# One plain feature tile instead of two, and eighteen early products instead of ten, in a Strassen-Winograd GeGLU kernel

## The chip, the cores and the metric

The kernel runs on one core of one Trainium2 chip. The metric is the device time of a run in microseconds (us). Most kernels' runs here lie within some 0.4% of each other, and only a comparison against the kernel before, run on the same chip in the same rounds, is used for small differences.

PE is the matmul engine (TensorE), PEld its weight loads, DVE is VectorE, ACT is ScalarE, POOL is GpSimd, SP is SyncE, which here only issues DMAs. `ps...` names are banks of PSUM, the memory that the matmuls write; SBUF is the memory that holds their operands.

## The reference

```python
# x: 1024 tokens x 1024, w_gate, w_up: 1024 x 3584, w_down: 3584 x 1024, all bf16
def reference(x, w_gate, w_up, w_down):
    return (gelu_tanh(x @ w_gate) * (x @ w_up)) @ w_down
```

## The kernel before

The features come in 28 tiles of 128. For each tile the kernel needs gate and up for 1024 tokens: plainly, 2 matrices x 2 token blocks x 8 depth steps = 32 matmuls of 128x512. Nearly all tiles are done by the Strassen-Winograd scheme instead. Depth and tokens are each cut in two, so w_gate gives the quadrants a11, a12, w_up gives a21, a22, and x transposed gives b11, b12, b21, b22. Seven products of four matmuls replace eight: 28 matmuls a tile. Its price is sums: s1 to s4 of weights (on DVE for the first pair, on POOL for all later ones) and t1 to t4 of x (on DVE), in fp32r, a 4-byte type.

A first few tiles stay plain, because they need no sums and can run while x and weights still arrive. Besides them, the product a12 x b21 (called P2) needs no sums either. It is computed early ("ahead") for some tiles, copied to SBUF, and added back when the tile's turn comes. Before, two tiles are plain and ten have P2 ahead. The code is shortened, and comments are added.

```python
FC = 2                       # tiles of a pair ("chunk")
NAHEAD = 10                  # tiles whose P2 is kept ahead
...
for k, eng in enumerate((nc.sync, nc.scalar)):        # start of the loads
    load_ahead(0, k, k + 1, eng)
for which, eng in enumerate((nc.sync, nc.scalar)):
    load_w(eng, 0, which, KD, KD + KQ)
load_xT(0, KD + KQ, DT)      # transposing DMA of x
load_ahead(0, KQ, KD)
load_w0(nc.sync, KD + KQ, DT)
load_ahead(1, 0, KD)
load_xT(0, 0, KD)
load_w0(nc.sync, 0, KD)
load_xT(1, 0, KD)
load_xT(1, KD, DT)
...                          # then w_up, w_gate of the first pair, last a12 rows
for ci in range(1, NCH):     # the pairs
    ...
    for fl in range(FC): prod(psc[fl], s1[fl], t1, True)    # the first product with sums
    for fl in range(FC): prod(psa[fl], s2[fl], t2, False)
    for st in open_fts: last_product(st)                    # a22r x t4 of the pair before
    for fl, ft in enumerate(fts): prod(psc[fl], s4[fl], b22r, False)
    if fts[0] < FC + NAHEAD: h0 = first                     # P2 was kept ahead
    else: ...                                               # P2 now, in a B bank
    begun = [first_product(ft + FC) for ft in fts]          # a11 x b11 of the next pair
    for fl, ft in enumerate(fts): prod(psa[fl], s3[fl], t3, False)
```

## Time and profile before

| | before |
|---|---|
| time, median | 275.52 us of the first 3 runs; 275.12 of the 6 that the change was compared with |
| profiled execution | span 273.2 us (time 274.97) |
| PE busy | 268.9 us, 98% |
| first pair: w_up and w_gate landed (issue plus time to landing) | 23.4 and 24.1 us |
| first pair: first weight load of a11 x b11 | 25.1 us |

These lines are from the page of the kernel before: busy time by engine, busy tenths in 40 slices, and the chain that ended last, by engine.

```profile
PE 268.9 (98%) x1202; PEld 188.4 (69%) x1202; DVE 193.8 (71%) x194; ACT 112.1 (41%) x183; POOL 107.1 (39%) x55
...
PE   8999999999999999999999999999999999999994
...
DMA  7994321423505505050514280005992445696202
...
PE 98%; ACT 0%; issue 0%
```

PE has work in every slice, and the chain from the last instruction back to the first is PE almost alone. So only fewer matmuls can make it shorter, and a new wait of PE makes it longer. DMA is fully busy only in the start, up to some 20 us, and from 191 to 205 us.

The table by stretches of 10 us, of the kernel before; after the length come busy us and instructions of PE, PEld, DVE, ACT and POOL, then the granted clock, the DMA share and GB/s. The DMA share sums the packets' own times, so it can exceed 1.

```profile
0.00:10.00 10.00, 9.23 (x43) 4.45 (x44) 1.27 (x3) 3.05 (x5) 0.70 (x6) 1.00 0.93 221
10.00:20.00 10.00, 10.00 (x48) 4.56 (x47) 5.09 (x6) 4.67 (x7) 0.00 (x0) 1.00 0.99 232
20.00:30.00 10.00, 10.00 (x47) 4.89 (x46) 9.16 (x8) 3.81 (x6) 0.00 (x0) 1.00 0.63 177
```

In the start both PE and DMA are full.

The chain in order of time, kernel before (start us, length us, what; L257 are products of the scheme, L272 the P2 ahead):

```profile
25.50 1.73 PE psA L257 x8
27.23 1.73 PE psC L272 x8
28.96 1.92 PE psC L257 x8
30.88 1.83 PE psA L257 x8
...
269.75 0.58 ACT o_sb L571
```

Eight bf16 matmuls take 1.73 us, 0.216 each; in the fp32r products eight take 1.81, 0.226 each. The piece at 28.96 is s1 x t1 of the first pair, the first product that needs sums. It divides the start from the rest (the timeline has its start at 28.77).

### The profile page before, as it was taken

The page shows a single profiled execution, that of the slowest core. Times are in us where ns is not written, and L with a number is a line of the kernel's source. Part 1 is how long each engine was busy: PE and PEld are TensorE (multiplying, and loading weights), DVE is VectorE, ACT ScalarE, POOL GpSimd, SP SyncE. Part 2 cuts the span into 40 slices and gives each one's busy share as a digit, 9 for nine tenths or more (in the row PEclk, how much of TensorE's full clock was granted, in tenths as well). Part 3 has the DMA queues.
Part 4 walks back from the last instruction along what each step waited for, and adds up shares of the span by engine and source line. Part 5 has one row for each costly group of instructions (what it writes and reads, how often), then busy time and mean ns, then how long its engine had stood idle before and what let it go on. Part 6 is the DMA issues. An engine that isn't in the chain of part 4 may idle for free.

```text
span 273.2 us, 3351 instructions
## 1 busy us (share of the span) xinstructions
PE 268.9 (98%) x1202; PEld 188.4 (69%) x1202; DVE 193.8 (71%) x194; ACT 112.1 (41%) x183; POOL 107.1 (39%) x55
## 2 busy tenths in 40 slices
PE   8999999999999999999999999999999999999994
PEld 4444777877877677676868686754447888888883
DVE  0268997986655676766658556459999999999511
ACT  2262665454643646555463636430300023962001
POOL 1000099999796794949577575000000000000000
PEclk9999999999999999999999999999999999999999
DMA  7994321423505505050514280005992445696202
GB/s 189 239 258 133 105 71 44 118 62 94 156 14 140 146 8 157 0 154 3 153 36 119 57 291 1 0 2 163 353 292 79 132 137 187 217 284 196 78 0 78
DMA packets 53249, 33.77 MB, mean 124 GB/s; under 512 B 8688, under 2 KB 53232, under 8 KB 53232
## 3 DMA queue, kind: packets, MB, share of 16 engines
q1 hardware_dynamic: 50240, 31.07, 39.7%
q10 hardware_dynamic: 2992, 2.49, 2.8%
q8 instruction: 9, 0.15, 0.2%
q14 instruction: 8, 0.07, 0.1%
HBM read 29.62 MB, written 2.10 MB: 116 GB/s over the span
## 4 chain that ended last, share of the span: by engine, by line
PE 98%; ACT 0%; issue 0%
PE psA L257 34%; PE psA L431 18%; PE psC L257 17%; PE psC L431 7%; PE psB L431 7%; PE psB L257 5%; PE psB L239 3%; PE psA L239 3%; PE psC L272 2%; PE psA L272 1%; PE psA L224 1%; PE tp L232 0%; ACT o_sb L571 0%
## 5 line engine op out<-in xcount | busy, mean ns | idle before, releaser
L257 PE MATMUL psA<-t,s 128*128 128x512 f32 x208 | 54.2, 402 | 0.0
L249 ACT ACTIVATE h<-c 128x512 bf16<-128x512 f32 x52 | 31.7, 627 | 37.4 <-DVE c L335 37.4
L257 PEld LDWEIGHTS psA<-t,s 128*128 128x128 f32 x208 | 39.1, 188 | 9.3
L162 POOL TENSOR_TENSOR s<-wu 128x1024 fp32r<-128x1024 bf16 x12 | 26.1, 2179 | 25.0 <-PE psC L257 16.8
L335 DVE TENSOR_TENSOR c<-sn,psA 128x512 f32<-128x512 f32 x26 | 17.7, 682 | 16.5 <-PE psA L257 14.6
L257 PEld LDWEIGHTS <-wg 128*128 128x128 bf16 x168 | 15.4, 98 | 20.2 <-issue 3.4
L163 POOL TENSOR_TENSOR s<-s,wg 128x1024 fp32r<-128x1024 f32 x12 | 27.4, 2284 | 0.9
L165 POOL TENSOR_TENSOR s<-wg,wu 128x1024 fp32r<-128x1024 bf16 x12 | 27.1, 2255 | 0.0
L340 ACT COPY sn<-psA 128x512 f32<-128x512 f32 x42 | 23.7, 584 | 7.9 <-PE psA L257 7.8
L257 PE MATMUL psA<-t,a22r 128*128 128x512 f32 x104 | 25.9, 391 | 0.0
L257 PE MATMUL psC<-t,s 128*128 128x512 f32 x104 | 25.8, 390 | 0.0
L257 PE MATMUL psC<-b22r,s 128*128 128x512 f32 x104 | 25.7, 389 | 0.0
L340 ACT COPY sn<-psC 128x512 f32<-128x512 f32 x26 | 15.2, 588 | 24.5 <-PE psC L257 22.7
L257 PE MATMUL psA<-b,wg 128*128 128x512 bf16 x104 | 24.6, 380 | 0.0
L257 PEld LDWEIGHTS psC<-t,s 128*128 128x128 f32 x104 | 19.4, 188 | 4.4 <-ACT ahead L362 0.3
L257 PEld LDWEIGHTS psA<-t,a22r 128*128 128x128 f32 x104 | 19.5, 188 | 4.1
L257 PEld LDWEIGHTS psC<-b22r,s 128*128 128x128 f32 x104 | 19.5, 188 | 4.1
L335 DVE TENSOR_TENSOR c<-sn,psC 128x512 f32<-128x512 f32 x26 | 17.7, 687 | 6.2 <-PE psC L257 6.2
L354 DVE TENSOR_TENSOR hi<-h,psA 128x512 bf16<-128x512 bf16 x14 | 9.6, 687 | 13.2 <-PE psA L257 13.2
L164 POOL TENSOR_TENSOR s<-wg,s 128x1024 fp32r<-128x1024 bf16 x8 | 17.2, 2155 | 0.6
L410 DVE TENSOR_TENSOR lo<-c,h 128x512 bf16<-128x512 f32 x12 | 16.9, 1405 | 0.6
L410 DVE TENSOR_TENSOR hi<-c,h 128x512 bf16<-128x512 f32 x14 | 16.9, 1205 | 0.5
(95 smaller groups left out, 398.5 us busy)
## 6 DMA issues: line engine op xcount, KB each, us to landing
wu<-in_w_up_dram SPq DMA_DIRECT2D x13, 512.0 KB, 4.1
wdb<-in_w_down_dram SPq DMA_DIRECT2D x12, 512.0 KB, 4.7
wdb<-in_w_down_dram SPq DMA_DIRECT2D x12, 384.0 KB, 4.2
wg<-in_w_gate_dram SPq DMA_DIRECT2D x8, 512.0 KB, 5.2
v<-in_w_down_dram SPq DMA_DIRECT2D x4, 512.0 KB, 6.1
out_dram<-o_sb ACTq DMA_DIRECT2D x16, 128.0 KB, 1.7
wg<-in_w_gate_dram SPq DMA_DIRECT2D x6, 256.0 KB, 4.5
v<-in_w_down_dram SPq DMA_DIRECT2D x4, 384.0 KB, 7.4
```

The lines of the kernel that those rows point to most:

```text
L162: yield eng.tensor_tensor(s1, a21, a22, ADD)
L163: yield eng.tensor_tensor(s2, s1, a11, SUB)
L164: yield eng.tensor_tensor(s4, a12, s2, SUB)
L165: yield eng.tensor_tensor(s3, a11, a21, SUB)
L239: nc.tensor.matmul(ps, lhsT=w_tiles[0, which][:, dt, fl * P : (fl + 1) * P], rhs=x_rows(dt, nb), start=(dt == first), stop=(dt == last),)
L249: nc.scalar.activation(h, src, ACT.Gelu_apprx_tanh)
L257: nc.tensor.matmul(ps, lhsT=lhs[:, k, :], rhs=rhs[:, k, :], start=(start and k == 0), stop=(k == KD - 1), skip_group_check=True,)
L335: tt(t, s, ps, ADD)
L340: nc.scalar.copy(t, ps)
L354: tt(g_of(ft)[:, :NB], h0, psa, MUL)
L410: tt(g_of(ft)[:, NB:], added(sn5[fl], psa[fl]), h1[fl], MUL)
L431: nc.tensor.matmul(banks[m], lhsT=lhs(k)[:, m * P : (m + 1) * P], rhs=rhs(k), start=(start and k == 0), stop=(k == HF - 1), skip_group_che ...
```

## The change

One tile less is plain, so one tile more saves its four matmuls. What PE loses in the start is made up by keeping P2 of eight more tiles ahead, eighteen in all. The results lie in SBUF rows of g that are not written yet (those of the first four in its lower half, the others in its upper half, as before), and the a12 rows of the later ten lie in slots of later sums. The 28 tiles become one plain tile, thirteen pairs and one last tile alone. The diff, cut to its core:

```diff
-    NCH = FT // FC
-    NAHEAD = 10
+    chunks = [range(0, 1)] + [range(f0, min(f0 + FC, FT)) for f0 in range(1, FT, FC)]
+    NCH = len(chunks)
+    NAHEAD = 18
...
+        a12_ahead += [
+            spool.tile([P, KD, KB * P], bf16, name="a12b", tag=t) for t in ("s2", "s4", "s3")
+        ]
...
         load_w0(nc.sync, 0, KD)
+        load_ahead(2, 0, KD)
+        load_ahead(3, 0, KD)
         load_xT(1, 0, KD)
         load_xT(1, KD, DT)
+        load_ahead(4, 0, KD)
+        for which in (1, 0):
+            load_w_all(1, which)
...
+        group_ahead(1, "CCAA", both)
+        for which in (0, 1):
+            plain(tok0[which], which, 0, 0, KD, KD, KD - 1)
+        plain_out(0, gelu(tok0[0], "h0", 4), tok0[1])
+        group_ahead(2, "CCAA", both)
+        tt(t1, b12, b11, SUB)
+        group_ahead(3, "CCAA")
...
-        nc.gpsimd.tensor_copy(ident[:, :1], t4[:, 0, :1])
+        nc.gpsimd.tensor_copy(ident[:, :1], s_tiles[1][2][:, 0, :1])     # before t4, waits for s3
...
-            if fts[0] < FC + NAHEAD:
+            if fts[-1] <= NAHEAD:
```

Cut here: the plumbing for a last chunk of one tile, the narrower loads of the plain tile's weights, and g's tiles being made when first used. The comment behind `s_tiles[1][2]` is added.

More of the change, by code (lines that the diff above doesn't have):

```diff
@@ L74, with g_tile @@
     ps1 = ctx.enter_context(tc.tile_pool(name="ps1", bufs=2, space=bass.MemoryType.PSUM))
+    def g_tile(name, b, dtype=bf16, cols=N):
+        k0, k1 = batches[b]
+        return gpool.tile([P, k1 - k0, cols], dtype, name=name, tag=f"{name[:2]}{k1 - k0}", bufs=2)
     def g_tiles(name, dtype, cols):
-        return [
-            gpool.tile(
-                [P, k1 - k0, cols],
-                dtype,
-                name=name,
-                tag=f"{name[:2]}{k1 - k0}",
-                bufs=2,
-            )
-            for k0, k1 in batches
-        ]
-    g_lo = g_tiles("lo", bf16, N)
+        return [g_tile(name, b, dtype, cols) for b in range(len(batches))]
+    ahead = [gpool.tile([P, KB, NB], fp32, name="ahead", tag=f"lo{KB}", bufs=2)]
+    g_lo = [g_tile("lo", b) for b in range(2)]
+    g_hi = []
     def by_batch(tiles):
@@ L98, in g_of @@
     def g_of(ft):
-        k = ft % HF
-        return by_batch(g_lo if ft < HF else g_hi)(k)
+        k, name, tiles = ft % HF, ("lo", "hi")[ft // HF], (g_lo, g_hi)[ft // HF]
+        if k in (k0 for k0, _ in batches[len(tiles) :]):
+            tiles.append(g_tile(name, len(tiles)))
+        return by_batch(tiles)(k)
     BANKS = {"A": 4, "B": 2, "C": 2}
@@ L117, in x_rows @@
         return ((b11, b12), (b21, b22))[dt // KD][nb][:, dt % KD, :]
-    ahead = [
-        gpool.tile([P, n, NB], fp32, name="ahead", tag=f"hi{n}", bufs=2) for n in (KB, KB, QF - KB)
-    ]
-    assert 2 * KB < NAHEAD <= KB + QF
+    ahead += [gpool.tile([P, n, NB], fp32, name="ahead", tag=f"hi{n}", bufs=2) for n in (KB, QF - KB) * 2]
+    ahead_at = [t[:, k, :] for t in ahead for k in range(t.shape[1])]
+    assert len(ahead_at) == NAHEAD and NAHEAD % FC == 0
     w_tiles = {}
@@ L131, in load_w, with a12_stays @@
     def load_w(eng, ci, which, d0, d1):
-        f0 = ci * FC * P
+        f0, n = chunks[ci][0] * P, len(chunks[ci]) * P
         src = (wg_r, wu_r)[which]
-        eng.dma_start(out=w_tiles[ci, which][:, d0:d1, :], in_=src[:, d0:d1, f0 : f0 + FC * P])
+        eng.dma_start(out=w_tiles[ci, which][:, d0:d1, :n], in_=src[:, d0:d1, f0 : f0 + n])
     def load_w_all(ci, which):
         alloc_w(ci, which)
-        load_w(nc.sync, ci, which, 0, KD if which == 0 and is_ahead(ci) else DT)
-    def is_ahead(ci):
-        return 0 < ci and (ci + 1) * FC <= FC + NAHEAD
+        load_w(nc.sync, ci, which, 0, KD if which == 0 and a12_stays(ci) else DT)
+    def a12_stays(ci):
+        return 1 <= chunks[ci][0] and chunks[ci][-1] < 1 + 2 * KB
     def quads(ci, fl=None):
-        cols = slice(None) if fl is None else slice(fl * P, (fl + 1) * P)
+        cols = slice(0, len(chunks[ci]) * P) if fl is None else slice(fl * P, (fl + 1) * P)
         wg, wu = w_tiles[ci, 0], w_tiles[ci, 1]
         a12 = wg[:, KD:, cols]
-        if is_ahead(ci):
-            i, j = divmod((ci - 1) * FC, KB)
+        if a12_stays(ci):
+            i, j = divmod(chunks[ci][0] - 1, KB)
             a12 = a12_ahead[i][:, :, j * P : (j + FC) * P][:, :, cols]
@@ L158, in sums @@
         s1, s2, s4, s3 = (
-            spool.tile([P, KD, FC * P], f32r, name=n, tag=n) for n in ("s1", "s2", "s4", "s3")
+            spool.tile([P, KD, FC * P], f32r, name=n, tag=n)[:, :, : len(chunks[ci]) * P]
+            for n in ("s1", "s2", "s4", "s3")
         )
@@ L165, in sums, with chunk_of @@
         yield eng.tensor_tensor(s3, a11, a21, SUB)
+    def chunk_of(ft):
+        ci = next(i for i, c in enumerate(chunks) if ft in c)
+        return ci, ft - chunks[ci][0]
     a22rs = {}
@@ L170, in a22r_of @@
         t = spool.tile([P, KD, P], f32r, name="a22r", tag="a22r", bufs=2)
-        nc.scalar.copy(t, quads(*divmod(ft, FC))[3])
+        nc.scalar.copy(t, quads(*chunk_of(ft))[3])
         a22rs[ft] = t
@@ L192, in load_ahead @@
         def load_ahead(i, k0, k1, eng=nc.sync):
-            f0, n = FC + i * KB, min(KB, NAHEAD - i * KB)
+            f0, n = 1 + i * KB, min(KB, NAHEAD - i * KB)
             eng.dma_start(
@@ L218 @@
         load_w0(nc.sync, 0, KD)
+        load_ahead(2, 0, KD)
+        load_ahead(3, 0, KD)
         load_xT(1, 0, KD)
         load_xT(1, KD, DT)
+        load_ahead(4, 0, KD)
+        for which in (1, 0):
+            load_w_all(1, which)
+        load_w_all(2, 0)
         warm_ps = acc("A")
@@ L235, with plain @@
                 (nc.vector.tensor_copy, nc.scalar.copy)[half](b21[:, dt, half * hw : (half + 1) * hw], tp)
-        def plain(ps, which, fl, nb, d0, d1, first=0, last=DT - 1):
+        def plain(ps, which, nb, d0, d1, first=0, last=DT - 1):
             for dt in range(d0, d1):
@@ L240, in plain @@
                     ps,
-                    lhsT=w_tiles[0, which][:, dt, fl * P : (fl + 1) * P],
+                    lhsT=w_tiles[0, which][:, dt, :P],
                     rhs=x_rows(dt, nb),
@@ L250, in gelu, with plain_out @@
             return h
-        def plain_out(ft, nb, h, up):
-            tt(g_of(ft)[:, nb * NB : (nb + 1) * NB], h, up, MUL)
+        def plain_out(nb, h, up):
+            tt(g_of(0)[:, nb * NB : (nb + 1) * NB], h, up, MUL)
         def prod(ps, lhs, rhs, start):
@@ L264, in prod @@
                 )
-        def ahead_of(ft):
-            i, j = divmod(ft - FC, KB)
-            return ahead[i][:, j, :]
         def product_ahead(ps, i, j, k0=0, k1=KD, cols=slice(None)):
@@ L279, in product_ahead, with group_ahead @@
                 )
-        ps = [acc(t) for t in "CCAA"]
-        tok0 = [(acc("A"), acc("B")) for _ in range(FC)]
-        def plain0(d0, d1):
-            for which in (0, 1):
-                for dt in range(d0, d1):
-                    for fl in range(FC):
-                        plain(tok0[fl][which], which, fl, 0, dt, dt + 1, KD, KD - 1)
+        def group_ahead(i, tags, copies=(nc.scalar.copy,)):
+            for j, tag in enumerate(tags):
+                ps = acc(tag)
+                product_ahead(ps, i, j)
+                copies[j % len(copies)](ahead_at[i * KB + j], ps)
+        ps = [acc(t) for t in "CCAA"]
+        tok0 = (acc("A"), acc("B"))
+        both = (nc.scalar.copy, nc.vector.tensor_copy)
         for k in range(KQ):
@@ L296 @@
                     product_ahead(ps[j], 0, j, k, k + 1, cols)
-        plain0(KD, KD + KQ)
-        for j, copy in enumerate((nc.scalar.copy, nc.vector.tensor_copy) * 2):
+        for which in (0, 1):
+            plain(tok0[which], which, 0, KD, KD + KQ, KD, KD - 1)
+        for j in range(KB):
             product_ahead(ps[j], 0, j, KQ)
-            copy(ahead[0][:, j, :], ps[j])
-        plain0(KD + KQ, DT)
-        a12_ahead.append(xpool.tile([P, KD, (NAHEAD - 2 * KB) * P], bf16, name="a12b"))
-        load_w_all(1, 1)
-        load_w_all(1, 0)
-        load_ahead(2, 0, KD)
-        load_w_all(2, 0)
-        for j, tag in enumerate("CCAA"):
-            ps = acc(tag)
-            product_ahead(ps, 1, j)
-            (nc.scalar.copy, nc.vector.tensor_copy)[j % 2](ahead[1][:, j, :], ps)
-        for fl in range(FC):
-            for which in (0, 1):
-                plain(tok0[fl][which], which, fl, 0, 0, KD, KD, KD - 1)
-            plain_out(fl, 0, gelu(tok0[fl][0], "h0", 4), tok0[fl][1])
-            if fl == 0:
-                tt(t1, b12, b11, SUB)
-        tok1 = [(acc("A"), acc("B")) for _ in range(FC)]
-        for fl in range(FC):
-            for which in (0, 1):
-                plain(tok1[fl][which], which, fl, 1, 0, KD)
+            both[j % 2](ahead_at[j], ps[j])
+        for which in (0, 1):
+            plain(tok0[which], which, 0, KD + KQ, DT, KD, KD - 1)
+        group_ahead(1, "CCAA", both)
+        for which in (0, 1):
+            plain(tok0[which], which, 0, 0, KD, KD, KD - 1)
[3 more added lines that the diff above has]
+        group_ahead(3, "CCAA")
+        tok1 = (acc("A"), acc("B"))
+        for which in (0, 1):
+            plain(tok1[which], which, 1, 0, DT)
+        tok1 = gelu(tok1[0], "h0", 4), tok1[1]
         tt(t2, b22, t1, SUB)
@@ L325 @@
             next(chunk1)
-        for fl in range(FC):
-            for which in (0, 1):
-                plain(tok1[fl][which], which, fl, 1, KD, DT)
-            tok1[fl] = gelu(tok1[fl][0], "h0", 4), tok1[fl][1]
         load_w_all(2, 1)
@@ L345, in first_product @@
                 psa = acc("A")
-                prod(psa, quads(*divmod(ft, FC))[0], b11, True)
-            if ft < FC + NAHEAD:
-                return psa, gelu(added(ahead_of(ft), psa), "h0", 4)
+                prod(psa, quads(*chunk_of(ft))[0], b11, True)
+            if ft <= NAHEAD:
+                return psa, gelu(added(ahead_at[ft - 1], psa), "h0", 4)
             return psa, snap(psa, "sn1")
@@ L358 @@
             prod(p1[fl], quads(1, fl)[0], b11, True)
-        for j, tag in enumerate("CC"):
-            ps = acc(tag)
-            product_ahead(ps, 2, j)
-            nc.scalar.copy(ahead[2][:, j, :], ps)
-        begun = [first_product(FC + fl, p1[fl]) for fl in range(FC)]
+        group_ahead(4, "CC")
+        begun = [first_product(ft, p1[fl]) for fl, ft in enumerate(chunks[1])]
         tt(t3, b22, b12, SUB)
         next(chunk1)
+        nc.gpsimd.tensor_copy(ident[:, :1], s_tiles[1][2][:, 0, :1])
         tt(t4, b21, t2, SUB)
-        nc.gpsimd.tensor_copy(ident[:, :1], t4[:, 0, :1])
-        for fl in range(FC):
-            plain_out(fl, 1, *tok1[fl])
+        plain_out(1, *tok1)
         open_fts = []
         for ci in range(1, NCH):
-            fts = range(ci * FC, (ci + 1) * FC)
-            if fts[0] == HF:
-                g_hi = g_tiles("hi", bf16, N)
+            fts = chunks[ci]
             if ci + 1 < NCH:
@@ L380 @@
                     pass
-            s1, s2, s3, s4 = ([s[:, :, fl * P : (fl + 1) * P] for fl in range(FC)] for s in s_tiles[ci])
+            s1, s2, s3, s4 = ([s[:, :, fl * P : (fl + 1) * P] for fl in range(len(fts))] for s in s_tiles[ci])
             sn5, sn2, h1, h0 = [], [], [], []
@@ L384 @@
             psc = [acc("C") for _ in fts]
-            for fl in range(FC):
+            for fl in range(len(fts)):
                 prod(psc[fl], s1[fl], t1, True)
                 sn5.append(snap(psc[fl], "sn5"))
-            for fl in range(FC):
+            for fl in range(len(fts)):
                 prod(psa[fl], s2[fl], t2, False)
@@ L398 @@
                 load_w_all(ci + 2, 1)
-            if fts[0] < FC + NAHEAD:
+            if fts[-1] <= NAHEAD:
                 h0 = first
             else:
-                for fl in range(FC):
+                for fl in range(len(fts)):
                     psb = acc("B")
@@ L406 @@
                     h0.append(gelu(added(first[fl], psb), "h0", 4))
-            begun = [first_product(ft + FC) for ft in fts] if ci + 1 < NCH else []
+            begun = [first_product(ft) for ft in chunks[ci + 1]] if ci + 1 < NCH else []
             for fl, ft in enumerate(fts):
```

## The prediction

> **What bounds it now.** TensorE. The page has PE busy 268.9 of 273.2 us (98%), and the chain of waits that ended last is 98% PE; in the table by ten-microsecond stretches PE is at 10.0 of 10 everywhere between 10 and 200 us, clock 1.00. The chain gives a 128x512 matmul as 1.73/8 = 0.216 us with bf16 operands and 1.81/8 = 0.226 us with the fp32r ones. Only fewer matmuls can help, and any new PE wait costs in full. The start is nearly a second limit: DMA is busy 0.93 and 0.99 in the first two stretches, and the weights of the first pair land at about 23.4 (w_up) and 24.1 us (w_gate), by issue times plus times to landing, when the first product of that pair loads its weights at 25.1 us: 1.0 us of slack.
>
> **What the change does.** One feature tile goes from the plain form (32 bf16 matmuls, 6.91 us) to the seven-product form (8 bf16 + 20 fp32r, 1.73 + 4.53 = 6.26 us): -0.65 us of PE. The eight further products kept ahead only move, from B banks in the later pairs to the start. The start keeps 104 matmuls before the first pair (72 + 32 for 40 + 64), so its PE time is unchanged, but its bytes are not: two more a12 loads of 512 KB, now ahead of the last two x transposes, and the 256 KB left of them ahead of the first pair's weights instead of behind them; the plain tile's weights shrink from 1 MB to 0.5 MB, in 256-byte rows.
>
> **Cost.** In the packet records of the start, packets of 1024, 512 and 256 bytes take 46, 27 and 18 ns at the median; over 16 engines a 512 KB a12 load is about 1.5 us, the 256 KB one 0.9, and the smaller plain weights save some 1.15. The Trainium skill, "DMA: Bandwidth & Descriptors", Specifications, says transfers under 512 bytes do read-modify-write; the only 256-byte packets of this trace are the transposes', so the saving may be smaller. Estimate: w_gate of the first pair lands at 24.1 + 3.0 + 0.9 - 1.15 = 26.8 us, and PE waits some 1.7 us for it (1 to 3), part of it taken earlier, at the first, second and third a12 groups. DVE's first sums move later with it.
>
> GpSimd may now start beside VectorE's last sum t4. Two-input SBUF sums do disturb each other (the low-half multiply: 0.69 us with POOL idle, median 1.76 beside it), which could hold a C bank of the second pair; I add 0.2 us. In the nine pairs without a B product, PE's period is about 10.8 us against some 9.5 of POOL and 8.5 of DVE, and before had five such pairs without PE waits, so I expect none. The lone last tile has B-bank and plain down-projection work between its steps: no wait. Down-projection unchanged.
>
> **Sum.** 275.5 - 0.65 + 1.7 + 0.2 = 276.7; since earlier partial overlaps may save something, I say 276.5 us, 80% range 274.5 to 278.7. Chances: faster by over 2% 0.01, within 2% 0.96, slower 0.03.
>
> **What would show it.** Steps right: PE idle of 1 to 3 us before 31 us, ended by DMA of wg or a12; first pair's s1 product starting 1 to 3 us later than 28.8; from there to the end about 0.65 us less than before once the 6.26 us and the moved products are counted; tail from the down-projection's start as long as before. Wrong: no PE idle in the start (then about 274.9), or PE waits on POOL sums or PSUM banks among the nine pairs.
>
> **What would make it wrong.** DMA faster than I sum; 256-byte rows much slower, or issue gaps (then over 278); DVE or POOL falling behind with nine tight pairs.

## The result, and the profile after

| | before | after |
|---|---|---|
| time, median of 6 runs | 275.12 us (274.88 to 275.63) | 276.76 us (276.42 to 277.01) |
| ratio | | 1.0056, 95% interval 1.0043 to 1.0069 |
| span of the profiled execution | 273.2 | 275.1 |
| s1 x t1 of the first pair starts (chain) | 28.96 | 31.68 |
| from there to the last output tile (chain) | 240.79 | 240.21 |

A ratio is the mean time of one kernel's runs over that of the other's runs of the same rounds, so it is not quite the ratio of the medians. The change made the kernel 0.56% slower, which counts as the same at 2% and is clear of noise.

The profiled execution of the changed kernel was its slowest run (277.01), so it overstates the start a little. Its chain in order of time (L272 are now the scheme's products, L283 the P2 ahead):

```profile
6.05 4.83 SPq L211
...
13.20 5.31 SPq L211
...
21.75 6.25 DMA wg<-in_w_gate_dram
28.00 0.05 issue
28.05 1.90 PE psA L272 x8
29.95 1.73 PE psC L283 x8
31.68 1.93 PE psC L272 x8
...
271.89 0.59 ACT o_sb L566
```

PE used to come here straight from other matmuls. Now the chain passes through a DMA: the first pair's w_gate, issued at 21.75, lands at 28.0, and only then does a11 x b11 begin. Before 21.75 it is SP alone, issue after issue (L211 are the transposes of x); how far that is SP and how far the bytes is taken up below. From s1 x t1 to the last output tile it is 271.89 - 31.68 = 240.21 us against 269.75 - 28.96 = 240.79, so 0.58 us are gained. The start lost 31.68 - 28.96 = 2.72. The difference of the spans, 1.9, is these two and 0.24 us of a shorter tail after the last output tile.

The part of the page after that answers to the chain's line of before:

```profile
PE 89%; SPq 7%; DMA 2%; issue 0%; ACT 0%
```

The stretches of the start, after:

```profile
0.00:10.00 10.00, 9.05 (x39) 4.37 (x40) 1.28 (x3) 2.92 (x5) 0.70 (x6) 1.00 0.84 190
10.00:20.00 10.00, 8.93 (x42) 3.70 (x41) 3.45 (x5) 3.92 (x6) 0.00 (x0) 1.00 1.02 229
20.00:30.00 10.00, 9.86 (x46) 4.31 (x45) 7.86 (x7) 5.32 (x7) 0.00 (x0) 1.00 0.89 200
```

PE now stands idle in the second and third stretch, where it did not before, and DMA has 2.6 us more to do in the third (0.89 of it instead of 0.63). What PE and its weight loads waited for in the first 32 us, after (engine, line, what ended the wait: us in total, times, longest):

```profile
PEld L283 <- DMA a12b<-in_w_gate_dram: 1.5, 1, 1.5
...
PE psC L283 <- DMA a12b<-in_w_gate_dram: 1.0, 1, 1.0
...
PEld L272 <- DMA wg<-in_w_gate_dram: 0.6, 1, 0.6
PEld L283 <- DMA a12a<-in_w_gate_dram: 0.6, 1, 0.6
```

These are all DMA: the third group of a12 rows (a12b), the first pair's w_gate, and the second group (a12a). A weight load runs ahead of its matmul, so the PE wait is the smaller of the two numbers where both are shown. Between 30 and 180 us the view of waits has none of PE on DVE, POOL or DMA, before or after. The 0.3 us by which a weight load waits for an ACT copy at s1 x t1 stand in both.

### The profile page after: what moved, and what is told of

It reads as the page before. It is cut to its first block, busy times and chain, and to the rows that moved or that the text cites. A ratio compares the mean times of both kernels' runs of the same rounds, so it can differ in the third digit from the quotient of the medians.

```text
span 275.1 us, 3363 instructions
## 1 busy us (share of the span) xinstructions
PE 269.7 (98%) x1198; PEld 189.9 (69%) x1198; DVE 199.1 (72%) x199; ACT 113.3 (41%) x185; POOL 114.3 (42%) x59
## 4 chain that ended last, share of the span: by engine, by line
PE 89%; SPq 7%; DMA 2%; issue 0%; ACT 0%
PE psA L272 35%; PE psA L426 18%; PE psC L272 18%; PE psC L426 7%; PE psB L426 7%; SPq L211 5%; PE psB L272 3%; DMA wg<-in_w_gate_dram 2%; SPq L200 1%; SPq L135 1%; PE psC L283 1%; ACT o_sb L566 0%; SPq L191 0%
## 5 line engine op out<-in xcount | busy, mean ns | idle before, releaser
L272 PE MATMUL psA<-t,s 128*128 128x512 f32 x216 | 56.5, 403 | 0.0
L272 PEld LDWEIGHTS psA<-t,s 128*128 128x128 f32 x216 | 40.6, 188 | 9.6
L164 POOL TENSOR_TENSOR s<-wu 128x1024 fp32r<-128x1024 bf16 (+1 forms) x13 | 27.7, 2134 | 19.4 <-DMA wu<-in_w_up_dram 14.2
L165 POOL TENSOR_TENSOR s<-s,wg 128x1024 fp32r<-128x1024 f32 (+1 forms) x13 | 28.3, 2176 | 1.0
L167 POOL TENSOR_TENSOR s<-wg,wu 128x1024 fp32r<-128x1024 bf16 (+1 forms) x13 | 28.3, 2176 | 0.0
L272 PE MATMUL psA<-t,a22r 128*128 128x512 f32 x108 | 27.0, 391 | 0.0
L272 PE MATMUL psC<-t,s 128*128 128x512 f32 x108 | 26.9, 390 | 0.0
L272 PE MATMUL psC<-b22r,s 128*128 128x512 f32 x108 | 26.7, 389 | 0.0
L272 PE MATMUL psA<-b,wg 128*128 128x512 bf16 x108 | 25.7, 380 | 0.1
L272 PEld LDWEIGHTS <-wg 128*128 128x128 bf16 x144 | 12.9, 98 | 17.7 <-issue 3.7
L272 PEld LDWEIGHTS psC<-t,s 128*128 128x128 f32 x108 | 20.2, 188 | 4.5 <-ACT ahead L296 0.3
L272 PEld LDWEIGHTS psA<-t,a22r 128*128 128x128 f32 x108 | 20.3, 188 | 4.3
L272 PEld LDWEIGHTS psC<-b22r,s 128*128 128x128 f32 x108 | 20.3, 188 | 4.2
L341 ACT COPY sn<-psA 128x512 f32<-128x512 f32 x36 | 20.6, 586 | 6.1 <-PE psA L272 5.8
L166 POOL TENSOR_TENSOR s<-wg,s 128x1024 fp32r<-128x1024 bf16 (+1 forms) x10 | 20.6, 2059 | 0.8
L405 DVE TENSOR_TENSOR lo<-c,h 128x512 bf16<-128x512 f32 x13 | 20.6, 1583 | 0.4
L469 ACT COPY snb<-psC 128x512 f32<-128x512 f32 x4 | 2.2, 590 | 34.5 <-PE psC L426 34.5
```

The source lines that it names most:

```text
L164: yield eng.tensor_tensor(s1, a21, a22, ADD)
L165: yield eng.tensor_tensor(s2, s1, a11, SUB)
L166: yield eng.tensor_tensor(s4, a12, s2, SUB)
L167: yield eng.tensor_tensor(s3, a11, a21, SUB)
L272: nc.tensor.matmul(ps, lhsT=lhs[:, k, :], rhs=rhs[:, k, :], start=(start and k == 0), stop=(k == KD - 1), skip_group_check=True,)
L341: nc.scalar.copy(t, ps)
```

## Experiments

Each table row is one kernel. "s1 x t1" is the start of that product in the timeline of the profiled execution, "rest" the span less that start. Single executions differ in the start: e9_t4wait has the changed kernel's start and 30.82 against 31.49. So the ratio decides; each is taken against runs of the kernel before in its own rounds.

| run | median us | ratio to before, 95% interval | s1 x t1 at | rest |
|---|---|---|---|---|
| before | 275.12 | 1 | 28.77 | 244.4 |
| after | 276.76 | 1.0056 (1.0043, 1.0069) | 31.49 | 243.6 |
| e1_noload | 275.34 | 0.9998 (0.9985, 1.0011) | 30.05 | 243.8 |
| e2_swap | 276.36 | 1.0040 (1.0026, 1.0054) | 31.58 | 243.6 |
| e3_early | 277.91 | 1.0090 (1.0074, 1.0106) | 32.16 | 243.6 |
| e4_both | 278.11 | 1.0102 (1.0086, 1.0117) | 30.68 | 244.6 |
| e5_noload2 | 275.12 | 1.0000 (0.9986, 1.0014) | 29.26 | 243.8 |
| e6_wide | 277.71 | 1.0089 (1.0070, 1.0109) | 32.01 | 243.7 |
| e7_ten | 279.67 | 1.0166 (1.0151, 1.0181) | 25.22 | 252.6 |
| e8_swap_act | 275.51 | 1.0013 (1.0001, 1.0025) | 29.46 | 244.1 |
| e9_t4wait | 276.37 | 1.0049 (1.0035, 1.0063) | 30.82 | 243.8 |
| e10_swap_act_t3 | 275.49 | 1.0013 (0.9999, 1.0027) | 29.69 | 243.9 |
| e11_swap_act_t3_split | 275.64 | 1.0018 (1.0002, 1.0034) | 29.71 | 244.1 |

The theory is that the start is bound by DMA and the added a12 rows make it longer, while the rest gains some 0.6 us. The rivals are that the order of matmuls, copies and banks in the start is at fault, or POOL's earlier start beside t4, or the nine pairs without a B product.

### Taking the added loads away

```diff
-        a12_ahead += [spool.tile(...) for t in ("s2", "s4", "s3")]
+        a12_ahead += [a12_ahead[1], a12_ahead[1], spool.tile([P, KD, KB * P], bf16, name="a12b", tag="s3")]
...
-        load_ahead(2, 0, KD)
-        load_ahead(3, 0, KD)
```

> Third and fourth groups of products ahead read the second group's rows instead of loading their own (wrong result on purpose, same instructions on PE): 1 MB less DMA in the start. Theory (the start is bound by DMA, everything after the start gained 0.6 us): no wait of PE for a12b, w_gate of the first pair lands near 25 us, the first pair's s1 product starts within 0.7 us of the 28.8 us it has in the kernel before, and the time is 274.2 to 275.0 us, 0.5 us or so under the kernel before. Rival (the start is later because of the order of the matmuls, copies and PSUM banks, or the loss lies in the nine tight pairs): time stays within 0.5 us of the changed kernel's 276.8.

Against the kernel before it measured 0.9998, while the changed kernel has 1.0056. So 0.58%, about 1.6 us, are these two loads, with every PE instruction in place. The rivals that leave the loads out of it fall. The result is wrong on purpose. The first pair's w_gate, issued at 17.74 here and at 21.75 in the changed kernel, took this long to land (KB, us), in this run:

```profile
wg<-in_w_gate_dram SPq DMA_DIRECT2D x1, 256.0 KB, 5.1
```

and in the changed kernel:

```profile
wg<-in_w_gate_dram SPq DMA_DIRECT2D x1, 256.0 KB, 6.2
```

So it landed at 22.9 instead of 28.0: in these two traces the two loads cost it 5.1 us, where the prediction had 3.0. Two issues, some 1 us of SP, went with them; that bytes alone cost time is shown by e6_wide below, which adds 512 KB and no issue. The expected time was missed by 0.3 us, and s1 x t1 came 1.3 us later than before instead of at most 0.7: the wait for a12b is gone, but waits for the rows that are still loaded stayed.

The waits of the weight loads in the first 34 us of this run:

```profile
PEld L279 <- DMA a12a<-in_w_gate_dram: 2.1, 2, 1.1
```

There are two of them: before the first group's second half, and before the second group (PE itself waited 0.6 and 0.5 us). With one plain tile, four matmuls fewer stand before each of these places, 0.86 us, and PE arrives before the load. The next run takes the second group's load away as well.

```diff
+        a12_ahead[1:] = [a12_ahead[0]] * 3 + [spool.tile([P, KD, KB * P], bf16, name="a12b", tag="s3")]
...
-        load_ahead(1, 0, KD)
```

> As the run without the third and fourth a12 loads, and the second group too reads the first group's rows (1.5 MB less DMA in the start, wrong result on purpose). That run came out 0.3 us above what was expected, with waits of 0.6 us each before the first group's second half and before the second group. Theory: the second of those goes, the first stays (its rows are still loaded), so the first pair's s1 product starts 0.4 to 0.6 us earlier than in that run and the time is 274.6 to 275.0 us. If no start wait were left, the gain of the plain tile would be the 0.6 us read from the chain. Rival (the early delay is not from loads but from the clock's warm-up or the copies): unchanged, 275.3.

The wait before the second group went, s1 x t1 came 0.8 us earlier in the profiled execution, but the median fell by 0.2 us only (275.34 to 275.12, just outside the expected 274.6 to 275.0) and the ratio is 1.0000; the intervals of the two overlap. So this run does not decide how much the early waits are worth. It does show the limit: with 1.5 MB less to load, the start is still 29.26 - 28.77 = 0.5 us longer than before (PE waits 0.54 us before the first group's second half), and the 0.6 us gained in the rest only pays for that.

### Are the loads in the wrong order?

Two moves were tried, each alone and both together. The first puts the last a12 rows behind the first pair's weights:

```diff
-        load_ahead(4, 0, KD)
-        for which in (1, 0):
+        for which in (0, 1):
             load_w_all(1, which)
+        load_ahead(4, 0, KD)
```

> Only the order of three loads: the first pair's w_gate and w_up ahead of the last a12 load (256 KB). Theory: w_gate lands about 2.5 us earlier, so the wait of 0.3 to 0.6 us just before the first product of the first pair goes, but the wait of about 1.2 us before the third a12 group stays; the last a12 load now lands near 28 us, about when it is wanted. Gain 0.2 to 0.5 us against the changed kernel, 276.2 to 276.6. Rival (that wait costs nothing because DVE's sums then bind): no change.

1.0040 against 1.0056, so about 0.4 us were gained, as expected, though the two intervals overlap. The wait for w_gate is gone from the view of waits and the one for a12b stays.

The second move brings the third a12 group, on PE and in the loads, ahead of the plain tile's second part:

```diff
         load_ahead(1, 0, KD)
+        load_ahead(2, 0, KD)
         load_xT(0, 0, KD)
         load_w0(nc.sync, 0, KD)
-        load_ahead(2, 0, KD)
...
         group_ahead(1, "CCAA", both)
+        group_ahead(2, "CCAA", both)
         for which in (0, 1):
             plain(tok0[which], which, 0, 0, KD, KD, KD - 1)
         plain_out(0, gelu(tok0[0], "h0", 4), tok0[1])
-        group_ahead(2, "CCAA", both)
```

> Only the third a12 group moved ahead of the plain tile's first-half products, in the loads and on PE. Theory: the wait before the third group goes (its 512 KB feed 3.5 us of PE, the 768 KB of x and plain weights moved behind it only 1.7 us), but the total of bytes ahead of the first pair's w_gate is unchanged, so PE waits at that product instead, for 1.2 to 1.8 us in place of 0.3: time within 0.3 us of the changed kernel, 276.5 to 277.0. Rival (each PE wait costs by itself): 1 us or more gained, 275.7.

> The orders of the two runs above together. Theory: the two waits are one shortage of bytes seen at two places, so only both moves together gain: about 1.2 us against the changed kernel, 275.3 to 275.8, more than the sum of the two alone. Rival (waits are independent): the sum of the two single gains.

Both missed. The order alone made it worse, 1.0090, and the two moves together worse still, 1.0102. For e3 the wait did move to w_gate as the theory says, but w_gate landed at 28.7 instead of 28.0. The stretch from 8 to 26 us, changed kernel (the last number is GB/s):

```profile
8.00:26.00 18.00, 16.93 (x78) 7.36 (x77) 8.28 (x9) 7.74 (x12) 0.00 (x0) 1.00 1.10 241
```

and e3_early:

```profile
8.00:26.00 18.00, 17.30 (x80) 7.65 (x80) 8.04 (x9) 8.19 (x13) 0.00 (x0) 1.00 1.11 207
```

The same list of loads in another order moves at 207 GB/s instead of 241. The loss does not lie where the third group was put: from 0 to 18 us the two runs move 209 and 210 GB/s. It lies behind, where the transposes of b12 and b22 and the loads after them run. From 18 to 26 us, changed kernel:

```profile
18.00:26.00 8.00, 8.00 (x38) 3.63 (x37) 4.82 (x4) 3.52 (x6) 0.00 (x0) 1.00 1.10 246
```

and e3_early:

```profile
18.00:26.00 8.00, 7.95 (x38) 3.53 (x38) 4.59 (x4) 4.94 (x8) 0.00 (x0) 1.00 0.97 185
```

Why the order does this was not tested, and there is one trace of each.

In e4, s1 x t1 did start 0.8 us earlier than in the changed kernel, yet nothing came of it. Its waits of the weight loads between 30 and 50 us:

```profile
PEld psC L272 <- POOL s L164: 0.7, 1, 0.7
PEld psA L272 <- POOL s L165: 0.6, 1, 0.6
```

These are the weight loads' waits; PE's own is 0.3 us. PE now runs into the second pair before POOL has summed its weights. POOL may start only after DVE's work for the first pair, and that starts when w_up lands: at 27.56 in this run, as late as before the two moves. So behind the wait for w_gate stands a second chain, w_up, DVE's sums, t4, POOL's sums, which binds as soon as PE comes earlier. In this profiled execution (277.23) the rest is 1.0 us longer than in the changed kernel. The other three runs took about 278.1, and none of them has a trace, so their further 0.9 us are unexplained.

### What the narrow rows save

The plain tile's weights are now loaded in rows of 128 columns. This run loads 256 again and leaves half unused:

```diff
+        n = FC * P if ci == 0 else n
         eng.dma_start(out=w_tiles[ci, which][:, d0:d1, :n], in_=src[:, d0:d1, f0 : f0 + n])
```

> The plain tile's weights are loaded with 256 columns a row again (512-byte pieces, half of them never used): 0.5 MB more, at the same packet count. Prediction's estimate: the narrow rows saved 1.15 us of DMA, so the time rises by 0.6 to 1.4 us over the changed kernel, to 277.3 to 278.2. Rival (a 256-byte row costs as much as one of 512[...]): no change, 276.5 to 277.0.

1.0089 against 1.0056 is 0.9 us, so the narrow rows do save; the prediction had 1.15. The runs of this kernel spread more (276.34 to 278.36), and the two intervals only just miss each other. The number of issues and of packets is that of the changed kernel, so these 0.9 us are bytes. The Trainium skill, "DMA: Bandwidth & Descriptors", Specifications, has read-modify-write below 512 bytes; a doubling of the cost that would cancel the smaller size is not seen here.

### Fewer products ahead

```diff
-    NAHEAD = 18
+    NAHEAD = 10
...
-        load_ahead(3, 0, KD)
-        load_ahead(4, 0, KD)
-        group_ahead(2, "CCAA", both)
-        group_ahead(3, "CCAA")
+        group_ahead(2, "CC", both)
...
-        group_ahead(4, "CC")
```

> One plain tile as in the changed kernel, but only ten products ahead as before, the other eight in their pairs: 1 MB and 32 matmuls less in the start. Theory: the products ahead are what PE does while the DMA brings x and the first pair; 32 matmuls are 6.9 us of PE, 1 MB is 3.0 to 3.3 us of DMA, so PE now waits longer: time 278.5 to 280.5. Rival (the added bytes are the whole loss, fewer of them help): 275.0 or less.

1.0166: as expected, this is far worse. The 32 matmuls belong later, 6.9 us, but s1 x t1 comes only 31.49 - 25.22 = 6.27 us sooner. PE waited for DMA before it (0.9 us for x and 0.9 for w_gate, by the timeline), and then for POOL; the rest is 252.6 - 243.6 = 9.0 us longer, 2.1 more than the matmuls moved there. Its PE waits on POOL, between 28 and 180 us:

```profile
PE psC L270 <- POOL s L164: 0.8, 1, 0.8
```

So the products ahead are not the fault in themselves. With one plain tile they are needed, and the trade is between what they bring PE to do and what their rows cost the DMA.

### POOL's earlier start

```diff
-        nc.gpsimd.tensor_copy(ident[:, :1], s_tiles[1][2][:, 0, :1])
         tt(t4, b21, t2, SUB)
+        nc.gpsimd.tensor_copy(ident[:, :1], t4[:, 0, :1])
```

> Only POOL's first wait put back from the last chunk sum to VectorE's t4, as before the change. Theory: in the changed kernel POOL's little copy already stands 2.1 us (0.2 before) while t4 runs[...], so POOL's sums begin at the same moment either way: 276.5 to 277.0, no change, and POOL's first real sum starts within 0.3 us of 37.7. Rival (the change let POOL start earlier and it matters, or t4 was slowed): 0.5 us or more of change.

1.0049 against 1.0056: no change. The timeline of the changed kernel, where t4 (L366) and POOL's copy (L365) meet:

```profile
35.45 2.28 DVE L366 TENSOR_TENSOR t<-b,t 128x2048 fp32r<-128x2048 bf16 x1
...
35.70 2.08 POOL L365 CAST ident<-s 128x1 bf16<-128x1 f32 x1 [34.39 <-DVE s L167]
...
37.74 2.14 POOL L164 TENSOR_TENSOR s<-wu 128x1024 fp32r<-128x1024 bf16 x1
```

and of the kernel before, where the copy waits for t4 and then runs:

```profile
34.09 0.19 POOL L368 CAST ident<-t 128x1 bf16<-128x1 f32 x1 [32.79 <-DVE t L366]
34.24 2.13 POOL L162 TENSOR_TENSOR s<-wu 128x1024 fp32r<-128x1024 bf16 x1
```

A copy of one column takes 0.19 us alone and 2.08 us beside t4, and t4 takes 2.28 us either way. POOL's first real sum follows t4 in both kernels. This agrees with the Trainium skill, "SBUF — State Buffer", Who interferes with whom, by which a VectorE instruction with two SBUF inputs and a GpSimd instruction that reads SBUF contend for a shared port pair, the loser blocked for the whole instruction. DVE was first, so the change's earlier permission for POOL is worth nothing.

### A better version?

The issue of the transpose of b11 holds SP for 4.83 us in the changed kernel, and the plain tile's next weights are issued only after it. This is no fixed time. SP's timeline of e5_noload2, which has 512 KB less issued before this transpose:

```profile
5.44 2.56 SPq L211 DMA_TRANSPOSE b<-in_x_dram  x1
```

of the changed kernel:

```profile
6.05 4.83 SPq L211 DMA_TRANSPOSE b<-in_x_dram  x1
```

and of e3_early, which has 512 KB more:

```profile
6.31 6.35 SPq L211 DMA_TRANSPOSE b<-in_x_dram  x1
```

So the long stretch of SP in the chain is in good part a wait for bytes issued before. In this try the weights go out from ACT's queue, between two copies, with the exchange of e2:

```diff
         load_xT(0, 0, KD)
-        load_w0(nc.sync, 0, KD)
...
             both[j % 2](ahead_at[j], ps[j])
+            if j == 0:
+                load_w0(nc.scalar, 0, KD)
```

> A try at a better version: the exchange of the last three loads as in the earlier run (0.4 us gained), and the plain tile's first-half weights issued on ACT's queue between two copies instead of on SP behind the transpose whose issue blocks SP for 5 us. Theory: the DMA idles about 0.5 us there; w and the third a12 group land 1 to 1.5 us earlier, the wait before the third group goes, and the time is 275.0 to 275.9, still not below the kernel before by more than 0.3 us. It could fail as the two-order run did: if w_up does not land earlier, DVE's sums and then POOL's bind, and the time stays at 276.4 or above.

1.0013, as expected: 0.7 us better than the exchange alone, and 1.2 us better than the changed kernel. The stretch from 10 to 14 us, in the changed kernel:

```profile
10.00:14.00 4.00, 3.94 (x19) 1.61 (x18) 1.38 (x2) 1.05 (x3) 0.00 (x0) 1.00 0.91 189
```

and in this run:

```profile
10.00:14.00 4.00, 3.63 (x17) 1.64 (x18) 0.72 (x2) 1.88 (x4) 0.00 (x0) 1.00 1.10 255
```

The DMA moves 255 GB/s where it moved 189 (170 in e2, the nearer comparison), and the wait for a12b is gone. What is left is a weight load's wait of 0.4 us on POOL in the second pair, where PE itself shows none, and 0.4 and 0.3 us of PE early in the start. The last two runs went after these, the first on top of e8, the second on top of the first:

```diff
         tt(t2, b22, t1, SUB)
+        tt(t3, b22, b12, SUB)
...
-        tt(t3, b22, b12, SUB)
         next(chunk1)
```

> The better version so far (275.5) with VectorE's sum t3 moved into its idle 1.1 us before w_up lands, ahead of the first pair's sums. Theory: there, PE waits 0.4 us for POOL's first sums, which start after t4; t4 now ends 0.7 us earlier, the wait goes, and the time is 275.0 to 275.3. Rival (that POOL wait is not what costs): 275.5.

```diff
-        load_ahead(0, KQ, KD)
+        load_ahead(0, KQ, KQ + 1)
+        load_ahead(0, KQ + 1, KD)
         load_w0(nc.sync, KD + KQ, DT)
-        load_ahead(1, 0, KD)
+        load_ahead(1, 0, KQ)
+        load_ahead(1, KQ, KD)
...          # and PE takes each half for four banks before the next
```

> As the run above, and the loads of the first group's second half and of the second group are each cut in two, with PE taking each half for all four banks as it lands. Theory: the two waits of 0.3 to 0.6 us left early in the start shrink by about half a load each; 274.4 to 275.0, below the kernel before. Rival (two more issues on SP delay all later loads by 1 us, and these bind): no gain or a loss, 275.2 to 276.2.

In e10 the wait on POOL is gone from the trace, but the ratio did not move, 1.0013; it had held up a weight load only. In e11 the two early waits are gone, and new ones of 0.27 us on x and 0.55 us on w_up stand right behind them; the ratio is 1.0018. Both missed what their theories gave and came out where their rivals had put them. No correct version beats the kernel before. The interval of e10 (0.9999 to 1.0027) just reaches it, those of e8 and e11 end just above it.

## Why the prediction was right

The prediction said 276.5 us and a range of 274.5 to 278.7; 276.76 was measured.

- **What bounds it.** Right. PE without waits was the whole chain before, and the added loads' waits showed in the time (e1). Not every wait was worth its length: e5 lost one of 0.5 us and 0.2 us of time.
- **-0.65 us for the tile.** Measured 0.58 us on the chain from s1 x t1 to the last output tile.
- **The start grows by DMA.** Right in kind, shown by e1, in which the two added loads account for 1.6 us of time. Its size was low: w_gate was to land at 26.8 us and landed at 28.0; the start was to grow by 1.7 us (1 to 3) and grew by 2.7 in the profiled execution. By the medians the start must have grown by about 1.64 + 0.58 = 2.2 us. The term that was mis-sized is the two a12 loads', 3.0 us, summed from packet medians as if the queue never paused. They cost w_gate 28.0 - 22.9 = 5.1 us against e1 (4.5 with the trace of e9, where w_gate lands at 27.3). The other two terms, 0.9 - 1.15 = -0.25, came to some -1.2 (24.1 to 22.9) and hid part of it. Where the queue loses the time was not settled. The 189 GB/s from 10 to 14 us are not the answer, though e8, which fills that place, gets 0.7 us back over e2: the kernel before has 207 there, and e1, without the loads, 193.
- **The total.** Partly luck. The prediction started from 275.5 us, the median of three runs, and the six runs have 275.12. Its terms add 1.25 us, and it said 1.0; measured are 1.64. The high base, and 0.2 us for POOL that did not come, made up for the start that was put too low.
- **Narrow rows save 1.15 us.** e6 gives 0.9.
- **0.2 us for POOL beside DVE.** Wrong in kind, too small to see. POOL's sums did not start beside t4 at all; POOL stood blocked, and e9 shows no effect.
- **No PE wait in the nine pairs.** Right for the changed kernel. The margin was not seen, however: in e4, e7 and e8 the second pair waits for POOL (in e8 a weight load only) when the start is shorter.
- **Where the waits stand.** They were predicted mainly at w_gate, partly earlier. In the trace the largest, 1.0 us, is at the third a12 group. The trace of e9, with the same loads, has 1.0 us in two waits at the first and second groups and 0.6 at the third, so the place varies from run to run. The e2, e3 and e4 runs were built on the belief that all these waits are one shortage of bytes. That belief fell for e3 and e4: in e3 the DMA moved fewer bytes from 18 to 26 us, and in e4 the chain through DVE and POOL was uncovered.

## What to carry to other kernels

Before trading matmuls against early loads, count bytes as well as matmuls for the stretch in which both PE and DMA are full: here 0.6 us of saved matmuls cost some 2 us of waiting, for 768 KB more ahead of the first pair's weights (1280 KB more of a12, 512 KB less of plain weights). In such a start, look at what the queue does between loads, and at which issue blocks the next, before changing their order; the order that reads better in the program can be slower. A wait taken away is worth only the distance to the next chain behind it, so look for that chain first.

## What the Trainium skill lacked or had wrong

- "DMA: Bandwidth & Descriptors", Issuing engines are not separate DMA queues, says that issuing from several engines only saves the sequencer's time, usually small beside the DMA itself. Here the issue of one 512 KB transpose held SP for 4.83 us (2.56 with 512 KB less issued before it, 6.35 with 512 KB more), and two issues moved to ACT were worth 0.7 us of the whole kernel (1.0040 to 1.0013); the rate from 10 to 14 us was 255 GB/s against 170.
- The same page, DMA Transpose (X-bar), has nothing on the time that the issue of a transpose takes (a cycle count for small tiles stands in the page's part on trn3), nor on the rate when transposes and copies follow one another in a queue; 185 GB/s were seen in e3 from 18 to 26 us, against 246 for the same loads in another order.
- The same page, Specifications, gives 512 bytes as the least size for line rate, and no cost below (the page's section Why small descriptors are slow has one, but no time of a packet). In the packet records here 256-byte packets took 18 ns at the median, 512-byte ones 27 and 1024-byte ones 46: dearer by the byte, cheaper by the row, so halving a row to 256 bytes still saved 0.9 us (e6).
- "SBUF — State Buffer", Who interferes with whom, was right and could say more plainly that even a copy of one column is held for the whole of the other engine's instruction: 2.08 us for 0.19.
- "TensorE: Matmul & The Clock Gate", Part 1, says that the warm-up point varies from run to run, which agrees: in the changed kernel's trace the 128x256 matmuls of the start ran at 0.21 us each up to 6.2 us, in e8's they were at half that from 4.4 us on. It puts the spread at 0.5 us either way; here the two are 1.8 us apart, though matmuls of different sizes make the point inexact. Whether this is part of the 0.7 us by which single executions differ in the start is not shown.
